# A third transposed-input buffer in dead key slots, a third mixer buffer, fewer buffers for VectorE's exponentials, and a new plan

## The chip, the cores and the metric

The kernel runs on one NeuronCore of a Trainium2 chip. TensorE (PE) multiplies matrices, VectorE (DVE) and ScalarE (ACT) work on whole tiles and read what TensorE left in PSUM, GpSimd (POOL) works on tiles in SBUF, and SyncE (SP) issues nearly all DMA transfers from one in-order queue. The metric is the device time of one execution in microseconds. Times of kernels are medians of several executions; a profile shows one execution.

## The reference

The input is one sequence of 2048 rows of 448 numbers. Two layers follow each other, each an attention block and a mixer with an MLP. In short:

```
for layer in (0, 1):                                  # the same weights in both
    a   = layernorm(x)                                # 448 wide
    qkv = a @ wqkv                                    # 16 heads of 28
    x   = x + (softmax(q k^T * 28**-0.5) v) @ wo
    y   = layernorm(x)
    h   = gelu(layernorm(y) @ w1)
    hs  = four groups of columns of h, shifted by +1, -1, +2, -2 rows, joined, @ w2
    x1  = y + hs
    x   = x + x1 + gelu(layernorm(x1) @ w3) @ w4      # w3: 448 x 1792, w4: 1792 x 448
```

Softmax over 2048 keys, for 2048 queries, 16 heads and two layers, is the largest piece of elementwise work: 134 million exponentials.

## The kernel before, in words

**Planned order.** The kernel is a set of small Python generators, one for each piece of work (`t_kv` loads and projects keys and values of a chunk, `t_q` queries, `t_scores`, `t_exp`, `t_pv`, `t_norm`, `t_outproj`, `t_mixA`, `t_mixB` and so on). `Sched.run` runs them while the program is being built. It keeps a clock for every engine from assumed durations, gives out buffers (`("acq", names)` asks for one, `("rel", name)` gives it back), and takes the operation that can start first or has the best rank. What comes out is one fixed list of instructions for each engine with semaphore waits between them. On the chip each engine works through its list in order, so that an instruction that waits holds up all that stand behind it in the list. `RANK` orders the pieces of work: ("k", layer, chunk) is key and value work, "q" queries, "a" output projection and first mixer half, "b" second mixer half with MLP. `Q_LEAD` says how many segments ahead of their use queries may be fetched. `D_RATE` is the share of score blocks that VectorE may take. `Sched.DOUBT` is a margin that the planner adds for TensorE behind a result of another engine.

**The stream of exponentials.** Attention is cut into segments of one layer, one chunk of queries (512 rows, or 256 for the last two chunks), one group of four heads and a range of keys. A block is 512 columns of scores for 128 keys and one head. Scores (L1212, four heads in four row strips of TensorE's array) go to PSUM banks 0 to 4, alternately three blocks and two. One ScalarE activation (L1367) takes the exponential of the three or the two blocks and writes them to PT. TensorE multiplies them by the values (L736, `ps<-PT,vaug`) into bank 5. Everything else that TensorE does is put between the scores of this stream. Where the planner sees TensorE idle, it puts in filler matmuls on the identity (L1783).

**Exponentials on VectorE.** A block may also go to VectorE, which has an exponential of five steps: `d_first` (L1253) out of PSUM into yd, then `d_chain` (L1274, L1276, L1278, L1281) by way of fb into one of `NPD` buffers PD. Such a block is taken only if a spare PSUM bank, a yd and a PD buffer are free at that moment, and only in chunks of four tiles.

**Transposed inputs.** All projections read a normalised and transposed input from one of two buffers `xT` (512 rows each). A piece of work acquires one, fills it by DMA transposes and holds it until its last matmul has been planned. `load_xT` (L996) transposes 512 rows from DRAM for keys or queries. `tr_dma` (L901) transposes one tile of 128 rows from SBUF, for the mixer halves `t_mixA` and `t_mixB` and for late key chunks. In the tail `tr_pe` (L912) does it on TensorE, evacuated by L919. `proj` (keys and queries), `v_proj`, `t_mixA` (w1) and `t_mixB` (w3) are the readers. Their matmuls carry the line of the helper, L745, or L736 where they are narrow. So a query projection appears as `L745 ps<-xT,wq_pad`, and its evacuation by VectorE as L1058; the correction of the queries is L1084.

**Mixer.** `t_mixB1` does one tile: w2 into PSUM, L1673 adds y into a buffer `x1b` (two of them, fp32), then statistics, norm (L896), a transpose, and a POOL addition L1688 that releases `x1b`. `t_mixB` projects with w3 for one to four tiles; VectorE moves the results to h2T (L1733), one long ScalarE activation (L1742) takes gelu of all, and w4 follows. Tables for gelu and back are loaded around it. After the last exponential (event "tail") gelu comes straight out of PSUM (L1729).

**Softmax denominators.** `t_norm` sends the row sums through small DMAs: L1460 (`rT<-ub`), reciprocal on VectorE (L1461), L1463 (`rscr<-rT`), L1468 broadcasts them back, and POOL multiplies (L1472).

**Keys.** kT holds 23 slots of 128 keys. Layer one (index 0) uses slots 0 to 15. Layer two uses 16 to 22 for its first seven tiles and then 0 to 8, when the event "kvfree" tells that layer one is through. Slots 9 to 15 of kT are dead then. In the text layer one and layer two are index 0 and 1.

Of the kernel before, what the change touches and what calls it, by code (L numbers as in the profile page):

```python
# [516 lines left out]
RANK = {k: round(1.1 + 0.05 * i, 3) for i, k in enumerate([('a', 0, 0), ('k', 0, 1), ('b', 0, 0), ('b', 0, 1), ('k', 1, 0), ('k', 0, 2), ('q', 0, 1), ('k', 0, 3), ('k', 1, 1), ('k', 1, 2), ('a', 0, 1), ('q', 0, 2), ('q', 0, 3), ('a', 0, 2), ('q', 1, 0), ('q', 1, 1), ('b', 0, 3), ('b', 0, 2), ('a', 0, 3), ('a', 0, 4), ('k', 1, 3), ('b', 0, 4), ('k', 1, 4), ('b', 1, 0), ('a', 1, 3), ('a', 1, 0), ('q', 1, 3), ('a', 1, 4), ('a', 1, 2), ('a', 1, 1), ('b', 1, 4), ('q', 1, 2), ('b', 1, 3), ('b', 1, 2), ('b', 1, 1)])}  # L517
Q_LEAD = {(0, 1): 4, (0, 2): 10, (0, 3): 3, (1, 0): 9, (1, 1): 8, (1, 2): 4, (1, 3): 3}
D_RATE = {(0, 0): 0.08, (0, 1): 0.05, (0, 2): 0.05, (0, 3): 0.13, (1, 0): 0.16, (1, 1): 0.1, (1, 2): 0.16}
# [10 lines left out]
Sched.DOUBT = {"dma": 1.0, "pool": 0.4, "dve": 0.05, "act": 0.2}  # L530
# [14 lines left out]
def build_kernel(nc, A_x, A_wqkv, A_wo, B_x, B_w1, B_w2, B_w3, B_w4, out, n_layers=2):  # L545
# [21 lines left out]
    NPD = 6  # L567
# [56 lines left out]
    with st:  # L624
# [24 lines left out]
        x1b = sb("x1b", [128, 2, D], FP32)  # L649
# [50 lines left out]
        xst = h2T[:, :, :].rearrange("p a b -> p (a b)").rearrange("p (t d) -> p t d", d=D)  # L700

# [197 lines left out]
        def tr_dma(slot, xt, i):  # L899
            k = num(slot)  # L900
            return dma("sp", lambda e: e.dma_start_transpose(out=xT[:, xt, :, 128 * i:128 * i + 128], in_=xn[:, k, :]),  # L901
                       reads=[("xn", k)], writes=[(("xT", xt), i)], t=TR_T, iss=1.2, touch=[slot])

        def tr_pe(slots, xt):
            n = len(slots)
            for h in range(0, n, 2):
# [9 lines left out]
                for i in range(m):  # L916
                    src = ps[:, bi(b), :].bitcast(BF16)[:, 512 * i:512 * i + 512].rearrange("p (f r) -> p f r", r=128)
                    dst = xT[:, xt, :, 128 * (h + i):128 * (h + i) + 128]
# [4 lines left out]
        def t_ln1_first():  # L923
            yield ("wait", ("setup",))
            x_ = yield ("acq", XT)
# [67 lines left out]
        def load_xT(L, t0, n, xt):  # L993
            for t in range(t0, t0 + n):
                yield ("wait", ("xnd", L, t))
            yield dma("sp", lambda e: e.dma_start_transpose(out=xT[:, xt, :, 0:128 * n], in_=xnd[128 * t0:128 * (t0 + n), :]),  # L996
                      reads=[("xnd", t) for t in range(t0, t0 + n)], writes=[(("xT", xt), i) for i in range(4)], t=TRL_T, iss=2.2)


        def proj(xt, g, wpad, wnm, NW=512):  # L1000
            b = yield misc(("xT", xt), (wnm,))
            for fc in FCS:
                yield op("pe", max(0.21, c_mm(NW)), mm4(ps[:, bi(b), 0:NW], wpad[:, fc, 128 * g:128 * g + 128], xT[:, xt, fc, 0:NW], fc == 0, fc == 3),
# [84 lines left out]
        def v_proj(L, c, xt):  # L1088
            yield ("wait", ("vinit",))
            t0, n = KC[L][c]  # L1090
            for i in range(n):
# [3 lines left out]
                for fc in FCS:  # L1095
                    yield op("pe", c_mm(D) + 0.0, mm4(ps[:, bi(b), 0:D], xT[:, xt, fc, 128 * i:128 * i + 128], wv[:, fc, :], fc == 0, fc == 3),
# [8 lines left out]
        def t_kv(L, c):  # L1105
# [3 lines left out]
            if L == 1 and c >= FASTKV:  # L1109
                yield ("wait", ("xns", t0))  # L1110
                x_ = yield ("acq", XT)
# [5 lines left out]
            else:  # L1117
                for t in range(t0, t0 + n):
                    yield ("wait", ("xnd", L, t))
                x_ = yield ("acq", XT, [("xnd", t) for t in range(t0, t0 + n)])  # L1120
# [11 lines left out]
        def t_q(L, qc):  # L1132
# [11 lines left out]
            x_ = yield ("acq", XT, [("xnd", t) for t in range(4 * qc, 4 * qc + 4)])  # L1144
# [418 lines left out]
        def t_mixA(L, tiles, direct, gname, pr):  # L1563
# [9 lines left out]
            x_ = yield ("acq", XT)  # L1573
# [11 lines left out]
            for grp in range(4):  # L1585
                b = yield misc(("xT", xt))
                for fc in FCS:
                    yield op("pe", c_mm(NW), (mm4 if NW > 300 else mm)(ps[0:112, bi(b), 0:NW], w1[:, fc, 112 * grp:112 * grp + 112], xT[:, xt, fc, 0:NW], fc == 0, fc == 3),
# [56 lines left out]
        def t_mixB1(L, t, i, xt, slots, direct):  # L1645
# [18 lines left out]
            x1s = yield ("acq", ["x10", "x11"], [k for rk in rks for k in rk])  # L1664
# [27 lines left out]
        def t_mixB(L, tiles, direct, pr):  # L1692
# [5 lines left out]
            x_ = yield ("acq", XT, [(("hT",), (0, tiles[-1] % HR))])  # L1698
# [23 lines left out]
            for fch in range(14):  # L1722
                b = yield misc(("xT", xt))
                for fc in FCS:
                    yield op("pe", c_mm(NW), (mm4 if NW > 300 else mm)(ps[:, bi(b), 0:NW], w3[:, fc, 128 * fch:128 * fch + 128], xT[:, xt, fc, 0:NW], fc == 0, fc == 3),
# [91 lines left out]
        for c in range(len(KC[1])):  # L1817
            SC.spawn(t_kv(1, c), RANK["k", 1, c])
            if c < 4:
                SC.spawn(t_q(1, c), RANK["q", 1, c])  # L1820
        SC.spawn(t_final(), 9)
# [58 lines left out]
```

## Time and profile before

| | |
|---|---|
| median of 4 executions | 1084.08 us (1082.73 to 1085.53) |
| the profiled execution, own time | 1085.53 us |
| its span, first to last instruction | 1083.7 us |
| mean granted TensorE clock | 0.991 |
| busy: TensorE, ScalarE, VectorE, POOL | 93%, 94%, 59%, 29% |
| exponentials on ScalarE (L1367) | 803, 919.5 us |
| first and last exponential | 23.09 us and 1029.34 us |
| blocks of exponentials on VectorE | 40 |
| filler matmuls (L1783) | 3860 |

Busy time is the share of the span in which an engine executes. The row of a group in the page gives the number of instructions, their busy time and mean, and the idle time of that engine just before them with what ended it. ScalarE's successive activations overlap a little in the records, so that means are longer than the pace at which they follow each other. The profiled execution was the slowest of the four.

### The profile page before, as it was taken

The page shows a single profiled execution, that of the slowest core. Times are in us where ns is not written, and L with a number is a line of the kernel's source. Part 1 is how long each engine was busy: PE and PEld are TensorE (multiplying, and loading weights), DVE is VectorE, ACT ScalarE, POOL GpSimd, SP SyncE. Part 2 cuts the span into 40 slices and gives each one's busy share as a digit, 9 for nine tenths or more (in the row PEclk, how much of TensorE's full clock was granted, in tenths as well). Part 3 has the DMA queues.
Part 4 walks back from the last instruction along what each step waited for, and adds up shares of the span by engine and source line. Part 5 has one row for each costly group of instructions (what it writes and reads, how often), then busy time and mean ns, then how long its engine had stood idle before and what let it go on. Part 6 is the DMA issues. An engine that isn't in the chain of part 4 may idle for free.

```text
span 1083.7 us, 35557 instructions
## 1 busy us (share of the span) xinstructions
PE 1011.5 (93%) x16114; PEld 426.5 (39%) x16117; DVE 642.5 (59%) x1250; ACT 1017.5 (94%) x922; POOL 315.7 (29%) x503
## 2 busy tenths in 40 slices
PE   6999899999989999989999999999998999899998
PEld 3333343443323244333433334353333343444465
DVE  7766578846578525675446652525685685554451
ACT  5999899999999999999998999999898999999952
POOL 3234125302264014453212210102524230432040
PEclk9999999999999999999999999999999999999999
DMA  4438211003121013221121232422322110121000
GB/s 128 122 94 225 79 56 32 19 21 90 32 31 31 12 57 78 49 31 27 35 85 41 44 79 92 136 62 95 61 42 36 38 44 13 32 65 30 2 20 32
DMA packets 92615, 62.27 MB, mean 57 GB/s; under 512 B 64688, under 2 KB 82368, under 8 KB 92464
## 3 DMA queue, kind: packets, MB, share of 16 engines
q1 hardware_dynamic: 89088, 51.92, 18.9%
q0 software_dynamic: 3376, 8.09, 2.7%
q8 instruction: 126, 2.06, 0.8%
q14 instruction: 25, 0.20, 0.1%
HBM read 27.12 MB, written 15.71 MB: 40 GB/s over the span
## 4 chain that ended last, share of the span: by engine, by line
ACT 67%; PE 21%; DVE 6%; DMA 3%; POOL 1%; issue 1%; SPq 0%; DVEq 0%
ACT PT L1367 61%; PE ps L745 11%; PE ps L1212 5%; PE ps L736 4%; ACT h2T L1742 3%; DMA xT<-xn 2%; DMA rT<-ub 1%; ACT fb L1616 1%; PE ps L1783 1%; DVE st L876 1%; ACT L1742 1%; ACT L1367 1%; DVE qT L1058 0%; POOL mst L1548 0%; DVE rT L1461 0%
## 5 line engine op out<-in xcount | busy, mean ns | idle before, releaser
L1367 ACT ACTIVATE PT<-ps 128x1536 bf16<-128x1536 f32 (+1 forms) x803 | 919.5, 1333 | 20.1 <-PE ps L1212 19.1
L1212 PE MATMUL ps<-qT,kT 32*128 32x512 bf16 (+1 forms) x2560 | 315.7, 342 | 36.1 <-ACT PT L1367 27.0
L736 PE MATMUL ps<-PT,vaug 128*32 128x512 bf16 (+1 forms) x2520 | 251.9, 343 | 0.2 <-DVE ub L1446 0.2
L1212 PEld LDWEIGHTS ps<-qT,kT 32*128 32x128 bf16 x2560 | 80.6, 91 | 311.4 <-ACT PT L1367 280.2
L1783 PE MATMUL ps<-ident 128*32 128x256 bf16 x3860 | 172.6, 277 | 6.0 <-DVE qT L1084 2.3
L745 PE MATMUL ps<-xT,w 128*32 128x512 bf16 (+2 forms) x2176 | 165.5, 363 | 6.0 <-DMA xT<-xn 4.9
L1783 PEld LDWEIGHTS ps<-ident 128*32 128x32 bf16 x3860 | 110.6, 97 | 38.1 <-issue 13.5
L1733 DVE CAST h2T<-ps 128x512 bf16<-128x512 f32 (+2 forms) x109 | 65.7, 603 | 80.2 <-PE ps L745 71.3
L736 PEld LDWEIGHTS ps<-PT,vaug 128*32 128x32 bf16 x2520 | 74.9, 95 | 93.4 <-issue 80.1
L745 PE MATMUL ps<-w,h2T 128*32 128x448 bf16 x1512 | 100.0, 354 | 9.2 <-ACT h2T L1742 9.2
L1472 POOL TENSOR_TENSOR otn<-ub,fb 128x512 bf16<-128x512 f32 (+1 forms) x36 | 41.6, 1156 | 152.8 <-DMA fb<-rscr 152.7
L745 PEld LDWEIGHTS ps<-xT,w 128*32 128x32 bf16 (+1 forms) x2176 | 59.4, 95 | 56.3 <-issue 30.1
L1011 POOL TENSOR_TENSOR sq<-kT 128x512 bf16<-128x512 bf16 (+2 forms) x32 | 30.3, 949 | 122.2 <-DVE kT L1025 122.1
L1614 POOL TENSOR_TENSOR fb<-hT 112x512 f32<-112x512 bf16 (+1 forms) x36 | 38.7, 1075 | 71.3 <-DVE hT L1596 54.3
L745 PEld LDWEIGHTS ps<-w,h2T 128*32 128x32 bf16 x1512 | 40.5, 96 | 42.9 <-issue 13.9
L745 PE MATMUL ps<-xT,wk_pad 128*32 128x512 bf16 (+2 forms) x576 | 49.7, 366 | 0.6 <-DVE qT L1058 0.4
L1688 POOL TENSOR_TENSOR x_res<-x_res,x1b 128x448 f32<-128x448 f32 x32 | 39.6, 1240 | 35.1 <-DVE xn L896 29.9
L1461 DVE RECIPROCAL rT<-rT 16x128 f32<-16x128 f32 (+1 forms) x36 | 33.6, 934 | 22.0 <-DMA rT<-ub 22.0
L1253 DVE TENSOR_SCALAR yd<-ps 128x512 int32<-128x512 f32 x40 | 27.1, 684 | 31.9 <-PE ps L1212 31.2
L1011 POOL TENSOR_TENSOR sq<-qT 128x512 bf16<-128x512 bf16 x28 | 29.7, 1067 | 48.7 <-DVE qT L1058 44.4
L745 PE MATMUL ps<-wv,xT 128*32 128x448 bf16 x512 | 42.2, 363 | 1.8 <-DVE kmaxc L1036 0.8
L745 PE MATMUL ps<-xT,wq_pad 128*32 128x512 bf16 x512 | 42.8, 382 | 0.1
(152 smaller groups left out, 1109.1 us busy)
## 6 DMA issues: line engine op xcount, KB each, us to landing
uscr<-ub SPq DMA_DIRECT2D x24, 256.0 KB, 2.9
ub<-uscr SPq DMA_DIRECT2D x24, 256.0 KB
fb<-rscr SPq DMA_DIRECT2D x24, 256.0 KB
xnd<-xn SPq DMA_DIRECT2D x28, 128.0 KB, 1.9
x_res<-in_A_x_dram POOLq DMA_DIRECT2D x16, 224.0 KB, 3.4
xd<-x_res SPq DMA_DIRECT2D x16, 224.0 KB, 3.1
x_res<-xd SPq DMA_DIRECT2D x16, 224.0 KB, 3.5
out_dram<-obf SPq DMA_DIRECT2D x16, 112.0 KB
```

What stands on the lines that cost most here:

```text
L736: return lambda e: e.matmul(out=out, lhsT=lhsT, rhs=rhs, start=start, stop=stop, **kw)
L745: r.append(e.matmul(out=out[c:c + w, :], lhsT=lhsT[:, c:c + w], rhs=rhs, start=start, stop=stop, tile_position=(0, c)))
L1011: return op("pool", 0.15 + NW * 0.0018, lambda e: e.tensor_tensor(out=sq[:, si, 0:NW], in0=src, in1=src, op=ALU.mult), reads=rk, writes=[( ...
L1212: yield op("pe", max(0.055, 0.22 / nc_ * NW / 512.0), lambda e, i=i, kc=kc, j=j, g=g, a=a, NW=NW, bank=bank: e.matmul(out=ps[:, bank, i * ...
L1367: yield op("act", 0.06 + n * w * 0.000833, lambda e, bk=bk, s0=s0, n=n, w=w: e.activation(out=PT[:, s0:s0 + n, 0:w], in_=ps[:, bk[0]:bk[0] ...
L1461: yield op("dve", 0.86, lambda e: e.reciprocal(out=rT[0:4 * n, :], in_=rT[0:4 * n, :]), reads=[("rT",)], writes=[("rT",)])
L1472: yield op("pool", 0.2 + NW * 0.0021, lambda e: e.tensor_tensor(out=otn[:, g, 0:NW], in0=u, in1=rb[:, 0:NW], op=ALU.mult), reads=[uk, fk], ...
L1614: yield op("pool", 0.2 + NW * 0.00165, lambda e: e.tensor_tensor(out=f, in0=z, in1=z, op=ALU.mult), reads=hk, writes=[fk])
L1688: yield op("pool", 1.2, lambda e: e.tensor_tensor(out=X, in0=X, in1=X1, op=ALU.add), reads=[xk, ("x1b", s)], writes=[xk], deps=[nop_])
L1733: ev = op("dve", c_ps(NW), lambda e, fch=fch, b=b: e.tensor_copy(out=hb[:, fch, 0:NW], in_=ps[:, bi(b), 0:NW]), reads=[("ps", bi(b))], wri ...
L1742: yield op("act", c_act(nl * NW), lambda e: e.activation(out=hb[:, 0:nl, 0:NW], in_=hb[:, 0:nl, 0:NW], func=ACT.Gelu_apprx_tanh), reads=al ...
L1783: return [e.matmul(out=ps[32 * c:32 * c + 32, bi(b), 0:256].rearrange("p (a n) -> p a n", n=128), lhsT=ident[:, 32 * c:32 * c + 32], rhs=i ...
```

## The change

`xv(xt)` gives buffer 0 or 1 of xT as before, and as buffer 2 the dead key slots 9 to 12 of kT. A new generator `t_third` waits for "kvfree", writes one column of them on POOL, which orders it behind all earlier readers of these slots, and signals "third". From then on `xts()` offers three buffers to all that acquire one. `x1b` gets a third buffer. `NPD` falls from 6 to 4. `RANK`, three `Q_LEAD`s, one `D_RATE` (chunk 3 of layer one) and the margin behind ScalarE are new, and so the planner puts out new lists for all engines. In counts of instructions: 37 blocks of exponentials on VectorE instead of 40, 805 activations on ScalarE instead of 803 (2011 blocks instead of 2008), 3736 filler matmuls instead of 3860, one POOL memset more; all else is the same number of instructions in another order, some of them on the new buffer.

```diff
-RANK = {k: round(1.1 + 0.05 * i, 3) for i, k in enumerate([('a', 0, 0), ('k', 0, 1), ('b', 0, 0), ('b', 0, 1), ('k', 1, 0), ('k', 0, 2), ('q', 0, 1), ('k', 0, 3), ('k', 1, 1), ('k', 1, 2), ('a', 0, 1), ('q', 0, 2), ('q', 0, 3), ('a', 0, 2), ('q', 1, 0), ('q', 1, 1), ('b', 0, 3), ('b', 0, 2), ('a', 0, 3), ('a', 0, 4), ('k', 1, 3), ('b', 0, 4), ('k', 1, 4), ('b', 1, 0), ('a', 1, 3), ('a', 1, 0), ('q', 1, 3), ('a', 1, 4), ('a', 1, 2), ('a', 1, 1), ('b', 1, 4), ('q', 1, 2), ('b', 1, 3), ('b', 1, 2), ('b', 1, 1)])}
-Q_LEAD = {(0, 1): 4, (0, 2): 10, (0, 3): 3, (1, 0): 9, (1, 1): 8, (1, 2): 4, (1, 3): 3}
-D_RATE = {(0, 0): 0.08, (0, 1): 0.05, (0, 2): 0.05, (0, 3): 0.13, (1, 0): 0.16, (1, 1): 0.1, (1, 2): 0.16}
+RANK = {k: round(1.1 + 0.05 * i, 3) for i, k in enumerate([('b', 0, 0), ('a', 0, 0), ('k', 0, 1), ('b', 0, 1), ('k', 0, 2), ('k', 1, 0), ('q', 0, 2), ('q', 0, 1), ('k', 1, 2), ('a', 0, 1), ('k', 0, 3), ('k', 1, 1), ('q', 0, 3), ('q', 1, 0), ('q', 1, 1), ('a', 0, 2), ('b', 0, 3), ('b', 0, 2), ('a', 0, 3), ('a', 0, 4), ('b', 0, 4), ('k', 1, 4), ('b', 1, 0), ('a', 1, 0), ('a', 1, 3), ('k', 1, 3), ('a', 1, 4), ('a', 1, 2), ('a', 1, 1), ('b', 1, 4), ('q', 1, 2), ('b', 1, 3), ('q', 1, 3), ('b', 1, 2), ('b', 1, 1)])}
+Q_LEAD = {(0, 1): 6, (0, 2): 10, (0, 3): 3, (1, 0): 7, (1, 1): 9, (1, 2): 4, (1, 3): 5}
+D_RATE = {(0, 0): 0.08, (0, 1): 0.05, (0, 2): 0.05, (0, 3): 0.06, (1, 0): 0.16, (1, 1): 0.1, (1, 2): 0.16}
...
-Sched.DOUBT = {"dma": 1.0, "pool": 0.4, "dve": 0.05, "act": 0.2}
+Sched.DOUBT = {"dma": 1.0, "pool": 0.4, "dve": 0.05, "act": 0.05}
...
-    NPD = 6
+    NPD = 4
...
-        x1b = sb("x1b", [128, 2, D], FP32)
+        x1b = sb("x1b", [128, 3, D], FP32)
...
+        def xv(xt):
+            return xT[:, xt, :, :] if xt < 2 else kT[:, :, 128 * 9:128 * 13]
+
+        def xts():
+            return XT + (["xT2"] if ("third",) in SC.events else [])
+
+        def t_third():
+            yield ("wait", ("kvfree",))
+            yield op("pool", 0.2, lambda e: e.memset(kT[:, :, 128 * 9:128 * 9 + 1], 0.0), writes=[("kT", g, s) for g in range(4) for s in range(9, 13)] + [("xT", 2)])
+            yield ("sig", ("third",))
...
-            yield dma("sp", lambda e: e.dma_start_transpose(out=xT[:, xt, :, 0:128 * n], in_=xnd[128 * t0:128 * (t0 + n), :]),
+            yield dma("sp", lambda e: e.dma_start_transpose(out=xv(xt)[:, :, 0:128 * n], in_=xnd[128 * t0:128 * (t0 + n), :]),
...
-            x_ = yield ("acq", XT, [("xnd", t) for t in range(4 * qc, 4 * qc + 4)])
+            x_ = yield ("acq", xts(), [("xnd", t) for t in range(4 * qc, 4 * qc + 4)])
...
-            x1s = yield ("acq", ["x10", "x11"], [k for rk in rks for k in rk])
+            x1s = yield ("acq", ["x10", "x11", "x12"], [k for rk in rks for k in rk])
...
+        SC.spawn(t_third(), 3)
```

In the same way every other `xT[:, xt, ...]` becomes `xv(xt)[...]` (`tr_dma`, `tr_pe`, `proj`, `v_proj`, `t_mixA`, `t_mixB`), and every other `("acq", XT ...)` becomes `("acq", xts() ...)` (`t_ln1_first`, `t_kv`, `t_mixA`, `t_mixB`).

## The prediction

> **What bounds the kernel now.** I read four views in this order: the page's busy times and chain of waits, ScalarE's waits, ScalarE's timeline, and then the timelines of the other engines at the places where ScalarE stood still.
>
> From the page, and then ScalarE's waits (us in total, times, longest):
>
> ```profile
> PE 1011.5 (93%) x16114; PEld 426.5 (39%) x16117; DVE 642.5 (59%) x1250; ACT 1017.5 (94%) x922; POOL 315.7 (29%) x503
> ACT 67%; PE 21%; DVE 6%; DMA 3%; POOL 1%; issue 1%; SPq 0%; DVEq 0%
> L1367 ACT ACTIVATE PT<-ps 128x1536 bf16<-128x1536 f32 (+1 forms) x803 | 919.5, 1333 | 20.1 <-PE ps L1212 19.1
> ...
> ACT PT L1367 <- PE ps L1212: 19.1, 16, 3.9
> ```
>
> ScalarE sets the pace: its 803 softmax exponentials (L1367) are 61% of the chain, and TensorE's scores (L1212) mostly wait for it. A change can therefore win in three places: work taken off ScalarE, the pauses in the exponential stream, and the tail after the last exponential. The first exponential starts at 23.09 us and the last one ends at 1029.34 us, so the tail is 1083.7 - 1029.34 = 54.4 us. The pauses are few. ScalarE's timeline (start, duration, group, count, idle before it) has nearly all of them:
>
> ```profile
> 112.53 2.37 ACT L1367 ACTIVATE PT<-ps 128x1536 bf16<-128x1536 f32 x2 [2.01 <-PE ps L1212]
> 115.87 70.42 ACT L1367 ACTIVATE PT<-ps 128x1536 bf16<-128x1536 f32 x62 [0.98 <-PE ps L1212]
> ...
> 342.88 2.54 ACT L1367 ACTIVATE PT<-ps 128x1536 bf16<-128x1536 f32 x2 [1.67 <-PE ps L1212]
> 346.13 36.60 ACT L1367 ACTIVATE PT<-ps 128x1536 bf16<-128x1536 f32 x32 [0.72 <-PE ps L1212]
> ...
> 575.88 26.04 ACT L1367 ACTIVATE PT<-ps 128x1024 bf16<-128x1024 f32 x23 [3.89 <-PE ps L1212]
> ...
> 773.40 1.02 ACT L1367 ACTIVATE PT<-ps 128x1024 bf16<-128x1024 f32 x1 [1.60 <-PE ps L1212]
> 775.35 4.64 ACT L1367 ACTIVATE PT<-ps 128x1536 bf16<-128x1536 f32 x4 [0.92 <-PE ps L1212]
> ...
> 821.11 2.42 ACT L1367 ACTIVATE PT<-ps 128x1536 bf16<-128x1536 f32 x2 [2.25 <-PE ps L1212]
> 824.07 20.99 ACT L1367 ACTIVATE PT<-ps 128x1536 bf16<-128x1536 f32 x18 [0.53 <-PE ps L1212]
> ```
>
> With 0.52 us more at 768.09 these are five places: P1 at 110 (2.99 us), P2 at 341 (2.39), P3 at 572 (3.89), P4 at 770 (3.04), P5 at 819 (2.78). In each, TensorE's in-order queue had stopped. The timelines of TensorE, VectorE and SyncE's queue say on what:
>
> ```profile
> 341.27 1.02 PE L1783 MATMUL ps<-ident 128*32 128x256 bf16 x24 [1.84 <-DVE x1b L1673]
> 771.80 1.02 PE L745 MATMUL ps<-xT,w 128*32 128x512 bf16 x8 [1.48 <-DMA xT<-xn]
> 819.69 0.83 PE L745 MATMUL ps<-xT,w 128*32 128x384 bf16 x8 [1.99 <-DMA xT<-xn]
> ...
> 562.49 1.30 SPq L996 DMA_TRANSPOSE xT<-xnd  x1
> 572.23 1.73 PE L745 MATMUL ps<-xT,wq_pad 128*32 128x512 bf16 x28
> 573.28 1.47 DVE L1058 TENSOR_SCALAR qT<-ps,bc 128x512 bf16<-128x512 f32 x2
> ```
>
> P3 differs from the others. TensorE is busy there, but with the 64 query matmuls of layer two's second chunk (569.20 to 573.96 us), whose evacuation by VectorE the very next scores need. Their transposed input was fetched only at 562.49 us, since both xT buffers were held until then. P4 and P5 wait for transposes on their way into xT, P2 for VectorE, P1 for VectorE behind a slow small transfer.
>
> **A rule against the trace.** After each of P1, P2, P4 and P5 the granted clock is halved (stretches of 1 us: busy of PE, PEld, DVE, ACT, POOL, then the clock):
>
> ```profile
> 819.00:820.00 1.00, 0.31 (x8) 0.17 (x8) 0.00 (x0) 0.00 (x0) 1.00 (x1) 0.83 0.00 0
> 821.00:822.00 1.00, 1.00 (x12) 0.23 (x9) 0.00 (x0) 0.89 (x1) 0.00 (x0) 0.50 0.00 0
> ```
>
> TensorE's own idle time before it was only 1.48 to 2.30 us. The Trainium skill, "TensorE: Matmul & The Clock Gate", section "HAM oscillation — how this bites in real kernels", puts the threshold at idle gaps above about 3.4 us. By that rule none of these pauses throttles, so the second pauses behind them (0.98, 0.72, 0.92, 0.53 us) would have other causes and would stay when the first is cured. By the trace they go together. I price by the trace and give the other sum below.
>
> **The change part by part.** The built order of the instructions shows what moves; positions below are the number of the exponential beside which an instruction stands. Orders differ from exponential 176 (about 235 us) on; only trifles differ earlier. So the start (23.1 us), a pause of 2.00 us at 33 us and P1 stay.
>
> 1. *Four PD buffers instead of six.* 37 blocks instead of 40 go to VectorE. ScalarE gets 3 more (402 x 3 + 402 x 2 + 1 = 2011 instead of 2008 blocks). In the chain 43 exponentials take 48.27 us, which is 1.123 each at 2.5 blocks, so 0.449 a block: +1.35 us, on the path. VectorE loses 3 x (0.68 + 0.72 + 0.84 + 0.52 + 0.73) = 10.5 us from the rows of L1253 to L1281; it is idle 41% of the span, so this counts at nothing except in P2.
>
> 2. *Third xT buffer (P3).* The fetch of these queries moves from exponential 436 to 409, into the new buffer, free from 402 on. Their matmuls move from 442-445 to 416-426, some 14 exponentials or 16 us before they are needed. P3 goes: -3.89. What is late next: 64 matmuls (4.8 us as they ran) now share the stretch with the up projection of the mixer, whose gelu waits longer. TensorE is idle 2.7 to 4.4 us in each 50 us there and fillers (L1783) can give way, so most is covered. I charge +0.5; without any cover it would be the 1.73 us of one burst, below nothing it cannot be. The memset that marks the buffer as free (POOL, 128x4) has no row; the nearest are POOL's small ones at 0.19 us. It waits for layer one's last readers of these keys; behind it on POOL stand the statistics of the next norm two exponentials later. From 0 to 1 us, hidden, since POOL is busy 29%: 0. SyncE issues as many transposes as before (64 and 13).
>
> 3. *P2.* L1673 stood behind three VectorE exponential steps (1.51, 1.25 and 1.64 us at 336 to 340 us, where the means are 0.84, 0.52 and 0.73) while POOL was adding. In the new order the same tiles' L1673 stand at 245 to 252 with no such step directly in front of the first three: -2.39.
>
> 4. *P5.* The late transpose was queued on SyncE behind the broadcast load L1468, which waits for a store to land. In the new order the transpose of that tile stands ahead of that pair, but still only four exponentials before its matmuls (632 to 636, before 636 to 640). Half: -1.39.
>
> 5. *P4.* Four exponentials between last transpose and matmuls become five (599 to 604). One transpose held the queue for 3.18 us instead of 1.22 here, and that may return anywhere. Half: -1.52.
>
> 6. *Tail.* TensorE's timeline after the last exponential:
>
> ```profile
> 1034.46 0.39 PE L1783 MATMUL ps<-ident 128*32 128x256 bf16 x8
> 1034.78 3.56 PE L736 MATMUL ps<-xT,w 128*128 128x256 bf16 x31
> ```
>
> From 1034.78 to 1080.8 us TensorE has work without a break. The new order puts 6 of these L736 matmuls ahead of the output projection and drops the 8 fillers: 6 x 0.115 + 0.32 = -1.0. ScalarE has one gelu of 6.18 us (another row of that form) instead of 4.89 + 1.86 there; it stays ahead of its reader. The three tail gelus that it does more before hT's (3 x 0.36) are matched by what TensorE does meanwhile.
>
> 7. *Third x1b buffer, new ranks and leads, a smaller safety margin behind ScalarE (0.2 to 0.05).* No instruction added. D_RATE of chunk (0, 3) acts on nothing, since only chunks of four tiles may use VectorE's exponentials. But many transfers and evacuations get new neighbours, and a plan can run into waits that it did not foresee, as four of the five places show. I count one new pause of their mean size, (2.99 + 2.39 + 3.04 + 2.78) / 4 = +2.8. From none to four is possible; no row says which.
>
> Sum: 1.35 - 3.89 + 0.5 - 2.39 - 1.39 - 1.52 - 1.0 + 2.8 = -5.5 us. The profiled execution took 1085.5 us (span 1083.7), so 1080.0. It was the slowest of four with a median of 1084.1; the comparison is between medians: 1084.1 - 5.5 = 1078.6. By the skill's rule only first pauses go (1.67, half of 2.25, half of 2.12) and a new one costs their mean of 2.0: -4.9, or 1079.2.
>
> **The rivals.**
>
> *A: pauses are dealt anew and the gain is eaten.* P3 goes, but two or three new pauses come, and P4 and P5 stay: 1.35 - 3.9 + 0.5 - 2.4 - 1.0 + 2 or 3 times 2.8 = 0 to +3. For it: four of five pauses come from transfers and queues that no plan foresaw. Against: P1 to P5 are all that 803 exponentials suffered above 1 us beside the start. With two it is no change: 1084.
>
> *B: slower, by VectorE in layer two's first mixer.* In the new order the stretch from exponential 614 to 634 holds the tanh steps, four PD blocks, L1673 of three tiles (which the third x1b buffer lets run at once) and the statistics of the next chunk. By the rows' means that is about 20% more VectorE work than time in 616 to 623 and 17% in 626 to 633: some 1.3 us late each. Every evacuation behind it is late, and TensorE stops as in P2. The fetch of queries for the third chunk and the transposes of the mixer hang on the same engine. It decides if more than three pauses of 2.8 us arise there and after, beyond the one counted: -5.5 + 3 x 2.8 = +2.9, or 1087. Against it: before has stretches as full (up to 24% over, at exponential 666) with no pause.
>
> *C: the third buffer does nothing in effect.* Matmuls moved earlier only push mixer work onto 443 and after, and P3 turns into a pause at the gelu: 1.35 - 1.0 - 0.4 = no change, 1084. TensorE's fillers before it (40 groups at exponentials 400 to 450) speak against.
>
> **How the numbers follow.** This kernel's times spread by 0.13% around their median, so about 0.2% (2.2 us) is what a measurement can tell from no change. My case: 0.62, from -12.8 (every pause from P2 on gone, the tail 1 us more, none new) to -2.2. A: 0.15 (0.09 of it within 2.2 us, 0.02 faster, 0.04 slower). B: 0.18. C: 0.05. Faster 0.64, same 0.14, slower 0.22. The range takes in most of my case, A, and half of B: 1070 to 1087.
>
> **What would show it.** Right: no pause over 1 us at the first scores of layer two's second chunk; L996 for it fetched at the start of layer two; 402 exponentials of 1024 columns; P1 still there with a clock of 0.50 behind it; about 1 us less from the last exponential to the end. Wrong: new pauses behind L1673 or L1733 in layer two, or a tail as long as before. If the pauses of ScalarE add up to more than 17 us again, the forecast fails in step 7.

## The result, and the profile after

The changed kernel takes 1079.92 us (median of 43 runs, 1076.74 to 1083.06) against 1082.37 us for the kernel before (64 runs, 1076.84 to 1091.54): a ratio of 0.9974, 95% interval 0.9966 to 0.9982, or 2.5 us by the medians and 2.8 us by the ratio. The forecast was -5.5 us, to 1078.6. The median of the four runs known then, 1084.08, lies 1.7 us above that of all 64.

Lines of the changed file stand 11 or 12 further down: L1367 is L1378 now, L1212 is L1223, L745 is L756, L736 is L747. The page and ScalarE's waits of the changed kernel:

```profile
PE 1005.8 (93%) x15990; PEld 422.4 (39%) x15993; DVE 635.2 (59%) x1238; ACT 1016.9 (94%) x921; POOL 316.5 (29%) x504
ACT 79%; PE 12%; DVE 6%; DMA 1%; issue 1%; POOL 1%; DVEq 0%; ACTq 0%
L1378 ACT ACTIVATE PT<-ps 128x1536 bf16<-128x1536 f32 (+1 forms) x805 | 919.9, 1331 | 15.4 <-PE ps L1223 14.7
...
ACT PT L1378 <- PE ps L1223: 14.7, 17, 3.2
```

ScalarE is busy as long as before. What fell is its idle time ahead of the exponentials, 20.1 to 15.4 us in its row. The timeline of ScalarE shows which pauses are left:

```profile
32.86 2.36 ACT L1378 ACTIVATE PT<-ps 128x1536 bf16<-128x1536 f32 x2 [2.00 <-PE ps L1223]
112.44 2.52 ACT L1378 ACTIVATE PT<-ps 128x1536 bf16<-128x1536 f32 x2 [3.17 <-PE ps L1223]
115.73 70.17 ACT L1378 ACTIVATE PT<-ps 128x1536 bf16<-128x1536 f32 x62 [0.77 <-PE ps L1223]
...
694.24 10.06 ACT L1378 ACTIVATE PT<-ps 128x1024 bf16<-128x1024 f32 x9 [2.67 <-PE ps L1223]
...
787.56 2.61 ACT L1378 ACTIVATE PT<-ps 128x1536 bf16<-128x1536 f32 x2 [0.72 <-PE ps L1223]
...
818.89 7.11 ACT L1378 ACTIVATE PT<-ps 128x1536 bf16<-128x1536 f32 x6 [1.10 <-PE ps L1223]
```

The second column is busy time, the brackets hold the idle time ahead of the group. P1 and the pause of the start stay. To compare the two kernels elsewhere, the pauses have to be matched by the number of the exponential, not by the time: P2 stands at exponential 262, P3 at 443, P4 at 600 to 606, P5 at 640. There the changed kernel has no pause left above 0.32 us. In their stead a pause of 2.67 us stands at 694 us (exponential 539), one of 0.72 us at 787 us (618) and one of 1.10 us at 819 us (644), four exponentials behind P5's place and ahead of other work. One profile is not enough to tell a pause of the plan from an accident of one execution, so the table has a second profile of both kernels and one of npd4, whose planned order is that of the kernel before (all below). The stream is the time from the start of the first to the end of the last exponential, and the last row is ScalarE's idle time within it:

| us | before | before_again | npd4 (same order) | after | after_again |
|---|---|---|---|---|---|
| span | 1083.7 | 1081.2 | 1081.1 | 1076.7 | 1078.8 |
| first exponential | 23.1 | 21.8 | 21.8 | 22.5 | 22.6 |
| stream | 1006.3 | 1005.0 | 1004.9 | 1001.0 | 1003.0 |
| tail | 54.4 | 54.4 | 54.4 | 53.2 | 53.2 |
| ScalarE idle in the stream | 20.5 | 19.4 | 19.4 | 15.2 | 17.1 |

On the means of these, the stream is 1005.4 - 1002.0 = 3.4 us shorter and the tail 1.2 us; 0.3 us of that is lost at the start, which the change hardly touches. That is 4.2 us of span, more than the 2.5 to 2.8 us of the medians: the executions that were profiled lay 1.4 us above the median on average for the order of before, and 0.4 us below it for the changed kernel. A profile tells where time goes, and can miss its amount by 1 to 2 us.

### The profile page after: what moved, and what is told of

Its sections match the earlier page's. It is cut to its first block, busy times and chain, and to the rows that moved or that the text cites. A ratio compares the mean times of both kernels' runs of the same rounds, so it can differ in the third digit from the quotient of the medians.

```text
span 1076.7 us, 35273 instructions
## 1 busy us (share of the span) xinstructions
PE 1005.8 (93%) x15990; PEld 422.4 (39%) x15993; DVE 635.2 (59%) x1238; ACT 1016.9 (94%) x921; POOL 316.5 (29%) x504
## 3 DMA queue, kind: packets, MB, share of 16 engines
q1 hardware_dynamic: 89088, 51.92, 18.3%
## 4 chain that ended last, share of the span: by engine, by line
ACT 79%; PE 12%; DVE 6%; DMA 1%; issue 1%; POOL 1%; DVEq 0%; ACTq 0%
ACT PT L1378 72%; PE ps L756 7%; ACT h2T L1753 4%; PE ps L1223 2%; PE ps L747 2%; ACT fb L1627 1%; DMA rT<-ub 1%; ACT L1753 1%; DVE st L887 1%; ACT L1378 1%; PE ps L1794 1%; DVE rT L1472 0%; DVE PD L1292 0%; DVE fb L1285 0%; DVE fb L1287 0%
## 5 line engine op out<-in xcount | busy, mean ns | idle before, releaser
L1378 ACT ACTIVATE PT<-ps 128x1536 bf16<-128x1536 f32 (+1 forms) x805 | 919.9, 1331 | 15.4 <-PE ps L1223 14.7
L1223 PE MATMUL ps<-qT,kT 32*128 32x512 bf16 (+1 forms) x2560 | 314.9, 341 | 34.0 <-ACT PT L1378 24.6
L747 PE MATMUL ps<-PT,vaug 128*32 128x512 bf16 (+1 forms) x2523 | 250.7, 342 | 0.0
L1223 PEld LDWEIGHTS ps<-qT,kT 32*128 32x128 bf16 x2560 | 80.6, 91 | 310.2 <-ACT PT L1378 282.8
L1794 PE MATMUL ps<-ident 128*32 128x256 bf16 x3736 | 166.9, 276 | 1.9 <-POOL ident L808 1.5
L1794 PEld LDWEIGHTS ps<-ident 128*32 128x32 bf16 x3736 | 107.8, 97 | 29.0 <-issue 12.1
L1744 DVE CAST h2T<-ps 128x512 bf16<-128x512 f32 (+2 forms) x112 | 67.9, 606 | 85.9 <-PE ps L756 78.0
L756 PE MATMUL ps<-xT,w 128*32 128x512 bf16 (+2 forms) x1376 | 109.6, 365 | 3.9 <-DVE h2T L1744 2.2
L747 PEld LDWEIGHTS ps<-PT,vaug 128*32 128x32 bf16 x2523 | 73.3, 95 | 94.9 <-issue 81.7
L756 PE MATMUL ps<-w,h2T 128*32 128x448 bf16 x1512 | 100.0, 359 | 10.4 <-ACT h2T L1753 10.4
L756 PE MATMUL ps<-kT,w 128*32 128x384 bf16 (+2 forms) x800 | 57.0, 352 | 2.7 <-DVE h2T L1744 2.0
L756 PEld LDWEIGHTS ps<-w,h2T 128*32 128x32 bf16 x1512 | 40.3, 97 | 45.4 <-issue 15.2
L756 PEld LDWEIGHTS ps<-xT,w 128*32 128x32 bf16 (+1 forms) x1376 | 37.9, 95 | 36.6 <-issue 18.5
L893 POOL TENSOR_SCALAR vpe<-mv 128x1 f32<-128x1 f32 (+2 forms) x21 | 5.5, 263 | 135.8 <-DVE mv L888 135.8
L756 PE MATMUL ps<-xT,wk_pad 128*32 128x512 bf16 (+2 forms) x512 | 44.1, 362 | 0.6 <-DVE qT L1069 0.4
L1753 ACT ACTIVATE h2T<-h2T 128x7168 bf16<-128x7168 bf16 (+2 forms) x8 | 42.0, 5244 | 0.1
```

Of the source, the lines that this page charges most:

```text
L747: return lambda e: e.matmul(out=out, lhsT=lhsT, rhs=rhs, start=start, stop=stop, **kw)
L756: r.append(e.matmul(out=out[c:c + w, :], lhsT=lhsT[:, c:c + w], rhs=rhs, start=start, stop=stop, tile_position=(0, c)))
L1223: yield op("pe", max(0.055, 0.22 / nc_ * NW / 512.0), lambda e, i=i, kc=kc, j=j, g=g, a=a, NW=NW, bank=bank: e.matmul(out=ps[:, bank, i * ...
L1378: yield op("act", 0.06 + n * w * 0.000833, lambda e, bk=bk, s0=s0, n=n, w=w: e.activation(out=PT[:, s0:s0 + n, 0:w], in_=ps[:, bk[0]:bk[0] ...
L1744: ev = op("dve", c_ps(NW), lambda e, fch=fch, b=b: e.tensor_copy(out=hb[:, fch, 0:NW], in_=ps[:, bi(b), 0:NW]), reads=[("ps", bi(b))], wri ...
L1753: yield op("act", c_act(nl * NW), lambda e: e.activation(out=hb[:, 0:nl, 0:NW], in_=hb[:, 0:nl, 0:NW], func=ACT.Gelu_apprx_tanh), reads=al ...
```

## The experiments

Two theories came first. Theory 1 was the prediction's: the third xT buffer cures P3 (the late queries of layer two's second chunk). Theory 2: the third x1b buffer does, since the mixer of layer one then lets go of its xT buffer sooner. A third: the new ranks do it, whatever the buffers. Four kernels, measured beside 21 runs of the kernel before (median 1082.90 us), part the three.

**x1b_only**

```diff
 # kernel before
-    NPD = 6
+    NPD = 4
-        x1b = sb("x1b", [128, 2, D], FP32)
+        x1b = sb("x1b", [128, 3, D], FP32)
-            x1s = yield ("acq", ["x10", "x11"], ...
+            x1s = yield ("acq", ["x10", "x11", "x12"], ...
```

> The kernel before with only the third x1b buffer, and four PD buffers instead of six to make room for it; two xT buffers, old ranks, leads and margin. In the planned order the queries of layer two's second chunk are fetched at exponential 412 and projected at 419 to 428, VectorE keeps 35 blocks. Theory 1 (the prediction's step 2: the third xT buffer cures pause P3): P3, 3.9 us at the first scores of that chunk, is still there in some form; with 5 blocks more on ScalarE (+2.2 us) the time is 0 to 3 us above before. Theory 2 (the third x1b buffer cures it): no pause over 1 us there, -3.9 + 2.2 = about 2 us below before, more if P2 goes too.

Measured: 1087.11 us, ratio 1.0046 (1.0021 to 1.0071). The time is in theory 1's direction, its profile is not. In ScalarE's timeline P2 and P3 are both gone, with two xT buffers and the old ranks; one pause of 2.56 us is at the place of the changed kernel's new one:

```profile
694.93 10.49 ACT L1367 ACTIVATE PT<-ps 128x1536 bf16<-128x1536 f32 x9 [2.56 <-PE ps L1212]
```

P4 is there, with 2.83 + 0.92 us at 772. The stream of this profile is 1002.2 us, like the changed kernel's, and the tail 58.1 us instead of 54.4. This execution was the fastest of seven (1083.79 us), and its span is only 0.9 us above that of before_again: the tail takes back what the stream gains, but the rest of the loss in the median is in no profile.

**two_xt**

```diff
 # changed kernel
-            return XT + (["xT2"] if ("third",) in SC.events else [])
+            return XT
```

> The changed kernel with only two xT buffers; three x1b buffers, new ranks, leads and margin stay. The planned order still fetches the queries at 409 and projects them at 416 to 426; VectorE keeps 34 blocks instead of 37. Theory 1 (third xT buffer): P3 returns and the time is about 3.9 + 1.3 us above the changed kernel, so about 2 us above before. Theory 2 (third x1b buffer): no P3, 1.3 us above the changed kernel for the three blocks, so 1 to 2 us below before.

Measured: 1083.42 us, ratio 1.0021 (1.0002 to 1.0040). There is no P3 here either, and at 695 us:

```profile
695.47 9.14 ACT L1378 ACTIVATE PT<-ps 128x1536 bf16<-128x1536 f32 x8 [3.28 <-PE ps L1223]
```

So the third xT buffer isn't needed to cure P3, and theory 1 falls as the explanation of it. Nevertheless the kernel is slower than the changed one by more than its three blocks cost. What else the third xT buffer is worth isn't shown: the profiled execution was the fastest of twelve (1080.33 us), and its span, 1078.5 us, is that of after_again.

**two_x1b**

```diff
 # changed kernel
-        x1b = sb("x1b", [128, 3, D], FP32)
+        x1b = sb("x1b", [128, 2, D], FP32)
-            x1s = yield ("acq", ["x10", "x11", "x12"], ...
+            x1s = yield ("acq", ["x10", "x11"], ...
```

> The changed kernel with only two x1b buffers; three xT buffers, four PD buffers, new ranks, leads and margin stay. In the planned order the queries are fetched at 425 and projected at 430 to 446, VectorE keeps 37 blocks. Theory 1 (third xT buffer): as fast as the changed kernel, 2 to 3 us below before. Theory 2 (third x1b buffer): most of P3 is back, at least 2 us above the changed kernel, so within 1 us of before or above it.

Measured: 1088.56 us, ratio 1.0065 (1.0045 to 1.0084), the slowest of all. P3 is gone here as well, so a third buffer of either kind cures it. But P2 is back (2.12 us at 342), the tail is 57.0 us, and before the last keys there is the longest pause of any kernel here:

```profile
700.26 9.14 ACT L1378 ACTIVATE PT<-ps 128x1024 bf16<-128x1024 f32 x8 [7.45 <-PE ps L1223]
```

**ranks_only**

```diff
 # kernel before, with RANK, Q_LEAD, D_RATE and Sched.DOUBT of the changed kernel
```

> The kernel before with only the new ranks, leads, rate and margin; all buffers as before. In the planned order the queries are fetched at 438 and projected at 443 to 445, VectorE keeps 37 blocks. If the new ranks are what gains (theory 3): 2 to 3 us below before. If the buffers are (theories 1 and 2): P3 is there with 3 to 4 us, and with three blocks more on ScalarE the time is 1 to 2 us above before.

Measured: 1087.05 us, ratio 1.0044 (1.0026 to 1.0061). P3 is there, longer (5.81 us), P2 too (1.69 + 0.68), and the tail is 58.3 us:

```profile
576.47 26.15 ACT L1367 ACTIVATE PT<-ps 128x1024 bf16<-128x1024 f32 x23 [5.81 <-PE ps L1212]
```

The new ranks alone lose. The third theory falls.

The next four runs take up what is lasting and what the PD buffers do (29 runs of the kernel before beside them, median 1082.35 us).

**before_again** (the kernel before, unchanged)

> The kernel before once more, for a second profile. If the five pauses come from the planned order they are all there again: P1 (3.0 us at 110), P2 (2.4 at 341), P3 (3.9 at 572), P4 (3.0 at 770) and P5 (2.8 at 819), each within 1 us. If P4 and P5, which wait for transposes on their way, are accidents of one execution, P1, P2 and P3 are there, P4 and P5 are under 1 us or elsewhere, and the span is 3 to 5 us shorter than 1083.7.

Measured: 1082.90 us in its one run, span 1081.2. All five pauses are there: P1 2.70 + 1.14, P2 1.30 + 1.13, P3 3.88, P4 0.67 + 0.75 + 0.64 + 0.54, P5 1.41 + 0.63. P4 and P5 belong to the plan too, but their size varies: TensorE waits for the same transposes, in this timeline for 1.26 and 1.70 us.

```profile
770.83 0.61 PE L745 MATMUL ps<-xT,w 128*32 128x512 bf16 x8 [1.26 <-DMA xT<-xn]
818.12 0.51 PE L745 MATMUL ps<-xT,w 128*32 128x384 bf16 x8 [1.70 <-DMA xT<-xn]
```

**after_again** (the changed kernel, unchanged)

> The changed kernel once more, for a second profile and for a comparison beside the other runs of this call. The pause of 2.7 us at 694 us comes from the planned order (all keys of layer two's last tiles must be projected before the next scores): it is there again within 0.5 us. The pause of 1.1 us at 819 is an accident and is gone or elsewhere. Time 2 to 3 us below before.

Measured: 1079.98 us, ratio 0.9985 (0.9971 to 0.9999). The pause at 694 us is again 2.67 us. The one at 819 was taken for an accident, and that was wrong: it is there with 3.18 us, and with 2.95 us in weights_later below, which has the same order. The matmuls of TensorE that stand still there are the mixer's first half for the next tile, reading the new third xT buffer (L756, `ps<-kT,w 128*32 128x512` in the program's names); the planned order has them three exponentials behind the last transpose into that buffer. The timeline names VectorE's h2T for 1.29 us in the first profile and no instruction for 2.30 us in the second, but that tile's transpose fits better. On SyncE's queue it stands behind a broadcast of softmax denominators, which waits for its store to land, as P5's did. From the changed kernel, then from both_mended (below), which has no pause there:

```profile
811.90 0.55 SPq L1479 DMA_DIRECT2D fb<-rscr  x1
812.82 1.23 SPq L912 DMA_TRANSPOSE kT<-xn  x1
...
808.83 0.56 SPq L1479 DMA_DIRECT2D fb<-rscr  x1
811.30 1.23 SPq L912 DMA_TRANSPOSE kT<-xn  x1
```

In the three profiles with the pause the transpose follows 0.6 to 0.9 us behind the broadcast, and the first matmul that reads it starts 4.7 to 5.6 us later; in keys_sooner and both_mended it follows 2.5 us behind, and the matmul starts after 3.3 us without waiting. No run moved this pair alone.

**xt_only**

```diff
 # changed kernel
+# RANK, Q_LEAD, D_RATE, Sched.DOUBT of the kernel before
-    NPD = 4
+    NPD = 6
-        x1b = sb("x1b", [128, 3, D], FP32)
+        x1b = sb("x1b", [128, 2, D], FP32)
-            x1s = yield ("acq", ["x10", "x11", "x12"], ...
+            x1s = yield ("acq", ["x10", "x11"], ...
```

> The kernel before with only the third xT buffer; two x1b buffers, six PD buffers, old ranks, leads and margin. In the planned order the queries of layer two's second chunk are fetched at 422 and projected at 428 to 444, VectorE keeps 39 blocks. If either third buffer cures P3 (as two_xt and two_x1b suggest): no pause over 1 us at 572, P2 still there (two x1b buffers), and a new pause before the last keys of layer two as in two_x1b (over 5 us at 700). If ranks that were chosen for other buffers cost by themselves, the time is above before, by 2 to 5 us, also by a longer tail (57 us or more instead of 54.4).

Measured: 1083.18 us, ratio 1.0015 (1.0001 to 1.0028). P3 is gone, P2 is there (1.31 us), and before the last keys stand 7.33 us, as expected. The longer tail isn't there (53.8 us), nor a time 2 us or more above before, so there is no sign that old ranks cost by themselves.

**npd4**

```diff
 # kernel before
-    NPD = 6
+    NPD = 4
```

> The kernel before with four PD buffers instead of six and nothing else. The planned order of all engines is the one of before: 40 blocks on VectorE, 3860 fillers. The prediction's step 1 charged the loss of three blocks (1.35 us) to the smaller number; if that were so, this kernel would be slower by 1.35 us or more. If six buffers were never in use at once: same time within 0.1%.

Measured: 1082.94 us, ratio 1.0013 (0.9994 to 1.0032). The interval holds no change and does not exclude the 1.35 us; but the planned order has the same 40 blocks and 3860 fillers as before, so that no block was lost to the smaller number. With six PD buffers the third x1b buffer doesn't fit in SBUF: that is what the four are for.

Put side by side, the pauses of layer two's beginning follow two positions in the planned order. The first scores of the second chunk stand at exponential 443 or 444, the first scores on the last three key tiles (13 to 15) at 542 or 543, in every kernel. The crowd in the last column but one is the largest number of key and value matmuls that TensorE has between two matmuls of scores there (670 to 712 us of each profile).

| kernel | query matmuls of chunk two | P3, us | last key tile transposed at | crowd, matmuls | pause before the last keys, us |
|---|---|---|---|---|---|
| ranks_only | 443 to 445 | 5.81 | 518 | 20 | none |
| before, before_again, npd4 | 442 to 445 | 3.89, 3.88, 3.89 | 526 | 20 | none |
| keys_sooner (below) | 416 to 426 | none | 528 | 20 | none |
| after, after_again | 416 to 426 | none | 531 | 36 | 2.67, 2.67 |
| x1b_only | 419 to 428 | none | 531 | 36 | 2.56 |
| two_xt | 416 to 426 | none | 531 | 48 | 3.28 |
| xt_only | 428 to 444 | none | 537 | 96 | 7.33 |
| two_x1b | 430 to 446 | none | 537 | 96 | 7.45 |

This is where most of P3's 3.9 us went. Every plan in which the queries come in time, up to here, lets the last key tiles come later, and what P3 gave is paid back there: 2.6 to 3.3 us with three x1b buffers, all of it and 3.5 us more with two. For these tiles layer one's mixer, the norm, a transpose and the projections follow each other. The later the transpose, the more projections are left to the same spot in TensorE's list, with no scores between them, and the pause grows with their number. The chain of waits of the changed kernel at that place has no ScalarE work in it from 689.32 to 694.24 us, 4.9 us; its end:

```profile
690.87 0.62 DVE vaug L1111
691.49 0.47 DVE kmaxc L1047
691.97 0.02 issue
691.99 0.17 DVE k L1172
...
692.72 0.54 DVE vaug L1111
693.26 0.04 issue
693.30 0.35 PE ps L756 x4
693.65 0.57 PE ps L1223 x5
694.22 0.02 issue
694.24 1.02 ACT PT L1378
```

Three kernels test this and P1 (29 runs of the kernel before beside them, median 1082.81 us), and a fourth puts both together.

**weights_later**

```diff
 # changed kernel, ahead of the loads of w3 and w4
-            yield ("wait", ("segstart", 9))
+            yield ("wait", ("st", 114))
```

> The changed kernel with the three loads of w3 and w4 (3.1 MB) moved on POOL's queue from exponential 64 to 114; the orders of TensorE, VectorE, ScalarE and SyncE stay what they are. P1 is put down to these loads: the 8 KB transfer of the first softmax denominators, issued at 102 us behind them, took over 6 us to land. If so, both pauses of P1 go (3.2 + 0.8 us) and the clock stays at 1.00 there: 3 to 4 us less than the changed kernel, 5 to 6.5 us below before. If the denominators' transfer is late by itself, P1 stays at 3 us or more and the time is that of the changed kernel. If the second pause and the halved clock come from something else than the idle before them, 0.8 us stay. A pause may come up instead at exponentials 114 to 128 (about 160 us), under 1 us by the gaps between the small transfers there.

Measured: 1082.55 us, ratio 1.0005 (0.9988 to 1.0021), so slower than the changed kernel. P1 is gone from its place, and a pause more than twice as long has come up at 164 us:

```profile
164.75 2.48 ACT L1378 ACTIVATE PT<-ps 128x1536 bf16<-128x1536 f32 x2 [5.62 <-PE ps L1223]
169.21 16.06 ACT L1378 ACTIVATE PT<-ps 128x1536 bf16<-128x1536 f32 x14 [1.99 <-PE ps L1223]
```

The timelines of POOL and SyncE and the chain of waits say why. POOL had nothing to do, came to the loads at 147 us, and the broadcast of the denominators, issued at 155.50 us into the same transfers, landed 6.70 us later; POOL's multiplication waited for it and TensorE for that:

```profile
148.71 1.12 POOL L801 DMA_DIRECT2D w<-in_B_w_dram  x1
162.28 1.26 POOL L1483 TENSOR_TENSOR otn<-ub,fb 128x512 bf16<-128x512 f32 x1 [12.45 <-DMA fb<-rscr]
...
155.50 0.53 SPq L1479 DMA_DIRECT2D fb<-rscr  x1
...
149.86 5.63 DMA rscr<-rT
155.49 0.02 issue
155.50 6.70 DMA fb<-rscr
```

The store ahead of that broadcast was held up as well, and by more: in both_mended, with no load on its way, the next transfer is issued 1.4 us after this store and POOL multiplies 5.1 us after the broadcast was issued, where it is 5.6 and 6.8 us here. So P1's cause is shown, and the expectation of a pause under 1 us failed.

**weights_later_before**

```diff
 # kernel before, the same edit
```

> The kernel before with the same loads moved in the same way, and nothing else; the orders of the other engines stay those of before. P1 goes (3.0 us), P2 to P5 stay: 2.5 to 3.5 us below before. If that holds here as in weights_later, the gains of the two changes add.

Measured: 1085.75 us, ratio 1.0036 (1.0022 to 1.0051). That is slower, not the 2.5 to 3.5 us faster that were expected. The same pair of pauses (5.63 + 1.98 us at 166) stands in place of P1; P3 is there with 3.89 us.

**keys_sooner**

```diff
 # weights_later, in RANK
-('a', 0, 4), ('b', 0, 4), ('k', 1, 4), ('b', 1, 0), ('a', 1, 0), ('a', 1, 3), ('k', 1, 3),
+('a', 0, 4), ('k', 1, 3), ('b', 0, 4), ('k', 1, 4), ('b', 1, 0), ('a', 1, 0), ('a', 1, 3),
```

> As weights_later, with one rank moved as well: keys of layer two's tiles 11 and 12 are ranked ahead of layer one's last mixer instead of behind layer two's first output projection. In the planned order the last key tile is transposed at exponential 528 instead of 531 (before 526, two_xt 531, two_x1b and xt_only 537); the first scores on these keys stand at 542 in all of them. If the pause at 694 is the chain to these keys being late, it falls from 2.7 us to about 0.5 to 1.5 (three exponentials are 3.4 us). If it is the crowd of projections that must run there whatever the transposes do, it stays at 2.7. What the later order does, which is planned anew from exponential 476 on, can add or take 3 us, also in the tail (53.2 us in the changed kernel).

Measured: 1079.10 us, ratio 0.9966 (0.9945 to 0.9987), 3.4 us below weights_later by the medians (the two intervals, 0.9945 to 0.9987 and 0.9988 to 1.0021, just part). The pause at 694 is gone, not only smaller, and the tail stays at 53.2 us. A pause of 2.15 us stands at 743 us, where weights_later has 0.79, and the 2.95 us of weights_later at 824 are not there. So the pause isn't there whatever the transposes do. But the crowd went with it: with the transpose three exponentials sooner, at most 20 key and value matmuls stand between two matmuls of scores, as before, instead of 36. The two belong together, and no run parts them.

**both_mended**

```diff
 # keys_sooner
-            yield ("wait", ("st", 114))
+            yield ("wait", ("st", 116))
```

> As keys_sooner, with the three loads of w3 and w4 behind layer one's fourth softmax multiplication on POOL's queue instead of just ahead of it (planned position 116 instead of 114; the orders of the other engines are those of keys_sooner). In weights_later and keys_sooner POOL came to the loads at 147 us, before the broadcast of the fourth denominators was issued at 155.5, and that broadcast then took 6.7 us: a pause of 5.3 + 2.0 us in place of P1. Behind the multiplication the loads can only start when that broadcast has landed. If that is the cause, there is no pause over 1 us at 110 nor at 164, and the time is 6 to 7 us below keys_sooner, 9 to 11 us below before. If the loads meet the next transposes (about 172 us), 1 to 3 us of that come back there.

Measured: 1070.67 us against 1082.71 (11 runs of the kernel before beside it), ratio 0.9889 (0.9865 to 0.9913): 12 us below before, 8.4 below keys_sooner by the medians. From ScalarE's timeline, in the part where P1 and the pause at 164 were, and its waits:

```profile
96.93 26.31 ACT L1378 ACTIVATE PT<-ps 128x1024 bf16<-128x1024 f32 x23
123.63 56.81 ACT L1378 ACTIVATE PT<-ps 128x1536 bf16<-128x1536 f32 x50 [0.39 <-PE ps L1223]
...
ACT PT L1378 <- PE ps L1223: 10.8, 15, 2.0
```

No pause above 0.39 us from 97 to 180 us. This is the fastest kernel of the study and beats the kernel before and the changed one. Its profile shows only part of the 8.4 us. The profiled execution took 1075.34 us, 4.7 us less than that of keys_sooner (1080.01): the pair of pauses at 164 is gone (5.25 + 1.98 us there), and at 738 to 744 us stand 1.73, 0.48 and 1.42 us where keys_sooner has 2.15 and 0.12. The six other executions took 1069.0 to 1071.4 us, at a mean granted clock of 0.997 or 0.998 instead of 0.992; what they lacked of these pauses is in no profile.

## Why the prediction was right or wrong

The direction held and the size was twice what came. The time lies in the range, but that was wide (1070 to 1087 us) and takes in the kernel before as well. By its steps:

1. *Four PD buffers, +1.35.* The three blocks more on ScalarE are real (805 activations); their reason was wrong. npd4 keeps 40 blocks with four buffers, and ranks_only has 37 with six: the new plan loses them, probably since the spare bank, yd and PD must be free at the right moment, which no run shows. The charge was too high for these profiles: the exponentials keep ScalarE busy for 920.0 us on the mean of two instead of 919.5 of three, +0.5.
2. *Third xT buffer, P3, -3.89 + 0.5.* P3 went in full. The fetch, at 562.49 us before, stands 36 us sooner and goes to the third buffer, as forecast:

```profile
526.92 1.98 SPq L1007 DMA_TRANSPOSE kT<-xnd  x1
```

   But that it takes the third xT buffer is where this step failed: x1b_only and two_xt cure P3 with two. Either third buffer suffices, and with the third xT buffer alone it does not pay (xt_only 1.0015). The term that was mis-sized is "what is late next". I looked for it at the mixer's gelu and charged 0.5 us; it is the last three key tiles, and costs 2.67 us in both profiles.
3. *P2, -2.39.* Right. P2 is there in every kernel with two x1b buffers (1.3 to 2.5 us for its first pause) and in none with three. With two, the last two of the four L1673 start at 339 to 343 us, behind eleven steps of VectorE exponentials; with three, all four have started by 329 us. This is the third x1b buffer's gain, which the prediction had put under new order.
4. *P5, half, -1.39.* At its place P5 went in full, 2.78 and 2.37 us in the two profiles of before (1.20 in npd4). But the pause four exponentials later, at 644, looks like the same thing again: a transpose queued close behind the same kind of broadcast. It counts in step 7; taken with it, half a credit was not too small.
5. *P4, half, -1.52.* The profiles of before's order have 3.04, 2.60 and 2.91 us at exponentials 600 to 606, the changed kernel 0.32 and 0.17 us: about -2.6, too small a credit. The third xT buffer isn't needed for it: ranks_only, with two, has 0.28 us at these exponentials, and x1b_only, also with two and with the old ranks, has P4 in full. The order decides here.
6. *Tail, -1.0.* Measured -1.2. TensorE's timeline has the six matmuls (3 and 3) where the order put them, ahead of the output projection, and no filler behind it:

```profile
1025.79 0.50 PE L747 MATMUL ps<-xT,w 128*128 128x256 bf16 x3
1026.22 0.71 PE L747 MATMUL ps<-rT,selq 8*128 8x128 f32 x4
1026.86 0.50 PE L747 MATMUL ps<-xT,w 128*128 128x256 bf16 x3
1027.30 1.70 PE L756 MATMUL ps<-wo_pad,otn 128*32 128x448 bf16 x32
1028.92 2.14 PE L747 MATMUL ps<-xT,w 128*128 128x256 bf16 x18
```

7. *One new pause, +2.8.* This is the term that was mis-sized. By exponential, in the two profiles of the changed kernel: 2.67 and 2.67 us at 539 (what step 2 called late next), 1.10 and 3.46 at 644, 0.89 and 1.08 at 618 to 620, 0.82 and 0.83 at 289, 0.58 and 0.86 at 161 to 166, 0.64 and 0.48 at 580, 0.55 and 0.52 at 690, 0.41 at 726 in one. None of them is in the kernel before; together about 7.7 to 9.9 us, where the sum had 2.8 and the 0.5 of step 2. The pauses at 289 and 618 have no larger one ahead of them: each comes at the end of 3.4 us in which the granted clock was 0.50.

So the four pauses named gave more than was credited (P2 to P5 sum to 12.1, 11.3 and 10.7 us in the profiles of before's order, of which 0.2 to 0.6 us stay; the credit was 3.89 + 2.39 + 1.39 + 1.52 = 9.2), and the new ones took back far more than the one counted. On the net, ScalarE's waits for scores sum to 19.1, 18.5 and 18.3 us in the three profiles of before's order and to 14.7 and 16.5 us in the two of after, under the 17 us that the prediction named as its sign of failure: 3.0 us less on the means, against 9.2 - 0.5 - 2.8 = 5.9 forecast. That is the missing half. In the stream as a whole ScalarE idles 3.6 us less, its exponentials take 0.5 us more and its other work 0.2 us less: 3.4 us less. With the tail (-1.2) and the start (+0.3) the profiles have -4.2; as said above, 1.8 us of that is which executions were profiled.

Rival A, that new pauses eat the gain, came half true. Rival B's place hardly stops: 0.89 and 1.08 us at exponentials 618 to 620. Of rival C the mechanism was there, though a hundred exponentials later than said: the pause moved rather than went.

The weighing of the clock rule isn't settled by more than the trace. Where a first pause was removed (P1 in both_mended), its second pause went too; where it grew (5.62 us in weights_later), the second grew with it, to 1.99 us. In the profile of both_mended the granted clock is 1.00 at 97 to 180 us. Where TensorE was busy for most of a pause (82% or more of it), on the other hand, the clock was not halved and no second pause came, however long the first: P3 (3.88 to 5.81 us) and the pauses before the last keys (2.56 to 7.45 us), although scores had been held up there too. All of that is for the trace's side, and speaks against held-up work as the only cause of a second pause. But no run changed the clock and nothing else.

## What to carry to other kernels

- In a kernel that streams on one engine, count its pauses and ask of each which instruction another engine's list had put too close. Then ask, before calling one cured, what deadline comes next on the same chain: here 3.9 us at the queries came back as 2.6 to 7.5 us at the last keys, until one rank moved their transpose forward by three exponentials and the projections no longer stood in one crowd ahead of the scores.
- Parts of a re-planned change do not add. Each of x1b_only, xt_only and ranks_only was slower than before (1.0046, 1.0015, 1.0044), and together they gained: here the ranks had to be chosen with the buffers that they rank for. An ablation of one part tells which pause it cures only if the profile is read pause by pause, tail included.
- Here a large load on a queue of its own still delayed the small transfers of another. Put it behind the instruction that uses the small transfer's result, not merely near it in the plan: moved two planned positions, 1079.1 became 1070.7 us.

## What was not expected of the hardware

A transfer of 8 KB for the denominators' reciprocals and one of 256 KB for their broadcast took over 6 us each while 3.1 MB of weights were on their way (6.48 us at 103.5 us in the kernel before, 6.70 us at 155.5 us in weights_later). The same steps without the loads are shorter: in weights_later the reciprocals of those first denominators start 3.6 us after their transfer was issued, and in both_mended POOL multiplies 5.1 us after the broadcast of the fourth. The small transfers lost most: 2.9 us or more at the reciprocals, 4.2 us at the store ahead of the broadcast, and 1.7 us at the broadcast itself.

The length of the tail follows TensorE's work in it. With 953 to 969 matmuls that end after the last exponential TensorE is busy for 50.0 to 51.0 us there and the tail is 53.2 to 54.4 us (after, two_xt, before, xt_only). With 998 to 1058 it is busy for 53.3 to 54.8 us and the tail is 57.0 to 58.3 us (x1b_only, two_x1b, ranks_only). Some of these matmuls are fillers. TensorE stands still for 3.0 to 4.2 us in all of them, so most of the difference is work that the plan has left for it.
